# Rounding on ScalarE, subtraction on GpSimd and new places for steps among the products: attention with two expert layers

## The chip, the cores and the metric

The kernel runs on one core of a Trainium2 chip. The metric is the device time of one execution in microseconds (us). Engines are named TensorE (PE, with its weight loads PEld), VectorE (DVE), ScalarE (ACT), GpSimd (POOL) and SyncE (SP, which issues most DMAs).

## The reference

Three stages follow each other; each one's output is the next one's input.

```
scores = scale * q @ k^T                      # 2 batches, 8 heads, 576 positions, head size 64
bias   = -(cum_i - cum_j), capped at 0        # cum: running sum of max(s, 0)
attn   = softmax(causal(scores + bias));  x = attn @ v      -> 1152 tokens x 512

first experts (8, 512->1024->512): each token goes to its best expert (softmax gate, at most
  288 tokens per expert); out = gate * (relu(x w1) w2)
second experts: the (token, expert) logits are served from the highest down, 144 tokens per
  expert, until each token has one; out = relu(x w1) w2
```

## The kernel before

**Attention.** The 16 heads run through a software pipeline written out by hand: one iteration m of a Python loop issues steps of several heads at once, in the order of `ORDER[m % 2]`, one list for even m and one for odd m. Names of steps: `M0` to `M3` (products of scores for the maxima of head m+3), `D0` to `D3` (VectorE takes the row maxima of them, line 485, into `rm`), `G0` (line 490: the five maxima of a row are scaled and rounded to whole numbers by adding and keeping the constant MAGIC), `G1` (line 497: VectorE takes MAGIC and the group references `refb` off, the result is `ng`; GpSimd then splits it into two f16 parts, `NH` at line 400 and `NL` at line 411, in `qb`), `Q` and `QE` (transpose of `qb` for head m+1, `br`), `E0` to `E3` (scores again, then exponentials on ScalarE, line 534, into `pf`), `P0` and `P1` (`ph`, the f16 part of `pf`, on VectorE, line 400; `pl`, the rest, on GpSimd, line 411), `V0` to `V2` (products with v into `pog`), `R0` to `R2` (row sums, reciprocal, scaling: lines 568, 571, 576), `T` and `TE` (transposes of k and q for head m+5, copied out by ScalarE as `al` and `ar`, line 406). Once for each pair of heads come `K`, `QS`, `VS`, `VT` (loads split in f16 parts; the second copy of the f16 part of q, `QD` at line 400, is GpSimd's), `S` (the low parts of k or q, line 438, VectorE) and `X1`, `X`, `XE`, `XG` (the output is split, `XR`, and multiplied with the gate). `D3` comes after `G0`: it reads the rounded `rm` as the start of its maximum (line 485, operand `rm`).

An even iteration holds `QS`, `VT` and the low part of q; an odd one `K`, `VS`, the low part of k and the GpSimd step on `XR`. A pair is one of each. All engines take their instructions in the order of the program.

**Second experts.** The 8 experts run one after the other (`moe2`). Each has a layer 1 (four groups of 24 f16 or bf16 matmuls, lines 904 to 906, each group followed by `relu` on ScalarE, line 915) and a layer 2 (four groups of f32 matmuls, line 1795, read out by ScalarE, line 1801). Which tokens an expert gets is worked out meanwhile, phase by phase, by the generator `work`: one `next(work)` runs one of seven steps of a phase. In short: `rows_of` (five transposes, line 1117, copied to `rowb` by ScalarE, line 1120), three steps of `compare` (ScalarE line 1532 for two of the five tiles, VectorE line 1534 for three), `products` (lines 1524 to 1540) with what follows from them on VectorE, the counts (line 1733, then VectorE from line 1736 on), and the slots (line 1394) with the choice of tokens. `layer1` and `second2` call `tick(k)` at 22 places of an expert (0 to 11 in layer 1, 12 to 21 in layer 2), and the tables `FIRST` (expert 0) and `THEN` (the others) say what is issued there: `w` a step of `work`, `h` the high part of a weight quarter (ScalarE, line 160), `l` its low part (VectorE, line 164), `0` and `1` the two halves of the previous expert's output (transposes at line 1811, ScalarE, a scatter by GpSimd at line 1815), `s` and `t` the two halves of the next expert's gathered input (16 transposes at line 1418, copied by ScalarE and by VectorE at line 1420), `.` nothing. `s` and `rows_of` write the same PSUM bank A0. After the last phase `checks` verifies the result: two multiplications on GpSimd, then eight short VectorE instructions.

Of the kernel before, what the change touches and what calls it, by code (L numbers as in the profile page):

```python
# [9 lines left out]
F32 = mybir.dt.float32  # L10
# [3 lines left out]
AF = mybir.ActivationFunctionType  # L14
OP = mybir.AluOpType
# [6 lines left out]
def tile_attention_moe_moe(ctx: ExitStack, tc: tile.TileContext, q, k, v, s, wg1, w1a, w2a, capacity,  # L22
                           wg2, w1b, w2b, out, dbg=None):
    nc = tc.nc
# [161 lines left out]
    ap = at.enter_context(tc.tile_pool(name="attn", bufs=1))  # L186
# [9 lines left out]
    NH = B * H  # L196
# [38 lines left out]
    RMS = [ap.tile([P, NT], F32, name=f"rm{i}") for i in range(4)]  # L235
# [91 lines left out]

    g1 = sp.tile([P, S], F32, name="g1")
    XB = ap.tile([P, NT, NH], F32, name="XB")
    refb = ap.tile([P, NH, G], F32, name="refb")  # L330

    def groups():
        nc.vector.tensor_scalar(g1[64:96], gi[64:96], 0.0, -1024.0, op0=OP.is_ge, op1=OP.mult)
        for r in (64, 96):
            nc.vector.scalar_tensor_tensor(BLS[0][r:r + 32, :S], gi[64:96], 31.0, g1[64:96], op0=OP.is_le, op1=OP.mult)
        for x in BLS[1:]:
            nc.gpsimd.dma_start(x[64:, :S], BLS[0][64:, :S])

    def references():
        ref8 = sp.tile([NH, G], F32, name="ref8")  # L340
        nc.vector.tensor_scalar(ref8, cum13[:, 0:S:32], 2.0 ** -10, MAGIC, op0=OP.mult, op1=OP.add)
        nc.vector.tensor_scalar(ref8, ref8, MAGIC, None, op0=OP.subtract)
        xrow = ones_row
        nc.vector.scalar_tensor_tensor(xrow.rearrange("e (g w) -> e g w", w=32),
                                       ref8[:, :, None].to_broadcast([NH, G, 32]), -1024.0,
                                       cum13.rearrange("e (g w) -> e g w", w=32), op0=OP.mult, op1=OP.add)
        nc.vector.tensor_copy(refh[:NH], ref8)
        r8l = sp.tile([NH, G], F32, name="r8l")
        nc.vector.tensor_sub(r8l, ref8, refh[:NH])
        nc.vector.tensor_copy(refh[32:32 + NH], r8l)  # L350
        pb = psM.tile([P, NT, NH], F32, name="pM")
        for t in range(NT):
            w = 128 if t < 4 else 64
            nc.tensor.transpose(pb[:w, t], xrow[:, t * P:t * P + w], identf[:NH, :NH])
        pr = psM.tile([P, NH, G], F32, name="pM")
        for h in range(NH):
            nc.tensor.matmul(pr[:, h], selc[:, h:h + 1].to_broadcast([64, P]), refh, start=True, stop=True)
        nc.scalar.activation(XB[:, :4], pb[:, :4], AF.Copy, scale=2.0 ** -13)
        nc.scalar.activation(XB[:64, 4], pb[:64, 4], AF.Copy, scale=2.0 ** -13)
        nc.scalar.activation(refb, pr, AF.Copy)  # L360


    wgh = const.tile([P, 4, 2, E], F16, name="wgh")
# [22 lines left out]
    def raw_copy(o, i):  # L386
# [2 lines left out]
    later = []  # L389

    ENG = dict(KL="DD", QL="DD", BR="DD", AL="AA", AR="AA", XE0="AA", XE1="AA", XH="AA",
               XL="PP", NH="PP", NL="PP", KH="AA", QH="AA", QD="PP", last="DD", PH0="DD", PH1="DD", PL0="PP", PL1="PP",
               VS="DD", VL="PP", VH="AA")

    def copied(name, i, o, x, scale=None):
        e = ENG[name][i % 2]
        if e == "A":
            nc.scalar.activation(o, x, AF.Copy, **({} if scale is None else dict(scale=scale)))
        elif scale is None:
            (nc.gpsimd if e == "P" else nc.vector).tensor_copy(o, x)  # L400
        else:
            (nc.gpsimd if e == "P" else nc.vector).tensor_scalar(o, x, scale, None, op0=OP.mult)
# [7 lines left out]
    def less(name, i, o, x, y):  # L410
        (nc.gpsimd if ENG[name][i % 2] == "P" else nc.vector).tensor_sub(o, x, y)  # L411
# [29 lines left out]
    def heads(m):  # L441
        n, h = divmod(m, 2)
        b, p = divmod(n, NP)
        return n, h, b, 2 * p + h
# [41 lines left out]
                                           r if t == 4 and j0 == 0 else -3e38, OP.add, OP.max, r)  # L486

    def q_dve0(m):
        rm = RMS[m % 4]
        nc.vector.tensor_scalar(rm[:, :NT], rm[:, :NT], 2.0 ** -10, MAGIC, op0=OP.mult, op1=OP.add)  # L490

    def q_dve1(m):
        n, h, b, hh = heads(m)
        rm = RMS[m % 4]
        qb = QB[n % 3]
        ng = aw.tile([P, NT, G], F32, name="ng")
        nc.vector.scalar_tensor_tensor(ng, rm[:, :NT, None].to_broadcast([P, NT, G]), MAGIC,
                                       refb[:, m, None, :].to_broadcast([P, NT, G]),
                                       op0=OP.subtract, op1=OP.subtract)
        copied("NH", m, qb[:, :, h, 64:64 + G], ng)  # L500
        less("NL", m, qb[:, :, h, 96:96 + G], ng, qb[:, :, h, 64:64 + G])

# [12 lines left out]
    def e_pe(m, u):  # L515
# [5 lines left out]
        for t, i0, i1 in EU[u]:  # L521
# [8 lines left out]
            r = OFF[t] + i0 - t * P  # L530
            todo.append((pf[:w, r:r + i1 - i0], o[:w], XB[:w, t, m:m + 1]))
            c += i1 - i0
# [55 lines left out]
    def xr(n, i):  # L588
        XR = XRP[1]
        b, p = divmod(n, NP)  # L590
        return XR[:, b, :, i * DM + p * P:i * DM + (p + 1) * P]

    def x1(n):
        xs = XSS[n % 2].rearrange("p t h d -> p t (h d)")
        copied("XH", n, xr(n, 0), xs)
        less("XL" if n < NPAIR - 1 else "last", n, xr(n, 1), xs, xr(n, 0))

# [147 lines left out]
    for m in range(-7, NH + 3):  # L745
# [51 lines left out]
        if m == -5:  # L797
            references()
# [767 lines left out]
    def pop_lo():  # L1566
        if late:
            split_lo(*late.pop(0))
# [22 lines left out]
    m, Bo = m0, Bo0  # L1591
# [168 lines left out]
    def checks():  # L1760

        nc.gpsimd.tensor_tensor(chk[:, 0], own0[:, 0], own0[:, 0], OP.mult)
        nc.gpsimd.tensor_tensor(chk[:, 1, :CT], SL2, SL2, OP.mult)
        nc.vector.reduce_sum(Q[:, 0, :E], chk[:, 0].rearrange("p t e -> p e t"), axis=AX.X)
        nc.vector.reduce_sum(Q[:, 1, :E], chk[:, 1, :CT].rearrange("p t e -> p e t"), axis=AX.X)
        nc.vector.reduce_sum(dbl[:, 0], BA0, axis=AX.X)
        nc.vector.reduce_sum(dbl[:, 1, :CT], A, axis=AX.X)
        nc.vector.memset(dbl[:, 1, CT:], 0.0)
        nc.vector.tensor_scalar(dbl[:, :2], dbl[:, :2], 1.5, None, op0=OP.is_ge)
        nc.vector.reduce_sum(Q[:, :2, E], dbl[:, :2], axis=AX.X)  # L1770
        nc.vector.tensor_add(Q[:, 2], Q[:, 0], Q[:, 1])
        yield
        pq = px[:, 128:128 + E + 1]
        nc.tensor.matmul(pq, onesf, Q[:, 2], start=True, stop=True)
        nc.vector.tensor_scalar(bad[:, 1, :E], tot, FULL, None, op0=OP.not_equal)
        nc.vector.memset(bad[:, 1, E:], 0.0)
        nc.vector.tensor_tensor(bad[:, 0], pq, expq, OP.not_equal)
        nc.vector.reduce_sum(badf, bad, axis=AX.XY)
        nc.vector.tensor_copy(badi, badf)
        nc.vector.tensor_scalar(badf, badf, 1e6, None, op0=OP.mult)  # L1780
        nc.vector.tensor_scalar(tokl, tok[:, E - 1], badf[:S2], None, op0=OP.add)
# [41 lines left out]
    def moe2(script):  # L1823
        pend = None
        given.difference_update(range(E, 2 * E))
        for e in range(E):
            i0 = 2 * E + 2 * e

            def tick(k, e=e):
                for c in script(e, k):  # L1830
                    if c == "h":
                        pop_hi()
                    elif c == "l":
                        pop_lo()
                    elif c in "01":
                        if pend is not None:
                            back2(*pend, int(c))
                    elif c == "w":
                        next(work, None)
                    elif e + 1 < E:  # L1840
                        XT1[e + 1] = spread(xg[e + 1], XT1.get(e + 1), "st".index(c))
                        if c == "t":
                            del xg[e + 1]
                    load_next()
                    gather_next()

            halved = HALF2 if e else 0
            hs = layer1(mo2, split_ws(i0), XT1.pop(e), CAP2, none, tick, halved)
            pend = (e, second2(i0 + 1, hs, halved, tick), gates[0])
            gates.pop(0)  # L1850
        last = []
        for q_ in range(2):
            back2(*pend, q_, last)
# [14 lines left out]

    FIRST = "w h lw l . 0ww ww . . . . w . ww h . l h wst lh lw1 hll"
    THEN = "w . . . 0 . . ww . w h l1w h wl . h l . swh tl l ."
    FIRST, THEN = (x.split() for x in (FIRST, THEN))
    next(work)
    pop_lo()
# [5 lines left out]
    pop_lo()  # L1881
    moe2(lambda e, k: (THEN if e else FIRST)[k].strip("."))
    assert next(work, None) is None
    bv = nc.values_load(badi[0:1, 0:1], min_val=0, max_val=4 * E)  # L1884
    with tc.If(bv > 0):
# [12 lines left out]
        def again(e, k):  # L1898
            if k == 8 and e + 1 < E:
                xg[e + 1] = gather(tok[:, e + 1])  # L1900
            return THEN[k].strip(".")

# [36 lines left out]
```

## Time and profile before

| | us |
|---|---|
| median of 3 runs | 489.27 (487.54 to 490.25) |
| profiled execution | 487.02 |
| its span, first to last instruction | 485.2 |
| busy: PE, PEld, DVE, ACT, POOL | 413.0, 380.5, 321.1, 244.4, 190.3 |

The attention takes the first 150 us, the products of the first experts run from about 163 to 276 us, those of the second from 327 to 472 us, and the first steps of the second routing lie between. A profiled instruction's line number is that of the kernel; a tile is named without its buffer number.

### The profile page before, as it was taken

Reading aid. Unit: us, or ns where it says so; the run is one execution under the profiler, and the core shown is the slowest. Engines: PE = TensorE matmul, PEld = TensorE weight load, DVE = VectorE, ACT = ScalarE, POOL = GpSimd, SP = SyncE. Lnnn points to the kernel's source line nnn. Section 1 sums busy time; section 2 is a strip of 40 time slices with the busy share of each in tenths; the row PEclk is TensorE's granted clock in tenths of the full one; section 3 lists DMA queues with packets and bytes.
Section 4 is the critical chain, followed back from the end, with each engine's and each line's share of the span. In section 5 each row is a group of like instructions: output and inputs, shape, how many; then the busy total and the mean of one; then the engine's idle time right before and its main releaser. Section 6 shows DMA issues by size and latency. Waiting matters only on the chain. (4 is left out here: it accounts for less than half of the span.)

```text
span 485.2 us, 13714 instructions
## 1 busy us (share of the span) xinstructions
PE 413.0 (85%) x5227; PEld 380.5 (78%) x5227; DVE 321.1 (66%) x949; ACT 244.4 (50%) x441; POOL 190.3 (39%) x299
## 2 busy tenths in 40 slices
PE   1679999977987999999999985649999999998980
PEld 1557778766774799999999985639899899998980
DVE  6799999995865357777778935458773763653300
ACT  3466777743662246545667604225456456454420
POOL 3595667756743503212322700432233322332211
PEclk9999999987987699999999988657999999999995
DMA  8787889749903689999996910449999769689001
GB/s 174 167 202 168 206 194 223 139 139 313 263 3 127 204 238 387 341 345 391 343 344 139 179 25 7 133 121 273 362 333 340 233 192 353 230 287 309 15 26 29
DMA packets 94405, 103.09 MB, mean 212 GB/s; under 512 B 56136, under 2 KB 63304, under 8 KB 94323
## 3 DMA queue, kind: packets, MB, share of 16 engines
q1 hardware_dynamic: 88931, 91.85, 65.3%
q0 software_dynamic: 4192, 9.91, 6.3%
q8 instruction: 45, 0.74, 0.6%
q10 hardware_dynamic: 1200, 0.30, 0.3%
q14 instruction: 37, 0.30, 0.2%
HBM read 81.42 MB, written 14.59 MB: 198 GB/s over the span
## 5 line engine op out<-in xcount | busy, mean ns | idle before, releaser
L164 DVE TENSOR_TENSOR wl<-wf,wh 128x1024 bf16<-128x1024 f32 x62 | 74.7, 1222 | 19.7 <-ACT wh L160 17.5
L160 ACT ACTIVATE wh<-wf 128x1024 f16<-128x1024 f32 x64 | 65.8, 1050 | 12.3 <-DMA wf<-in_moe_w_dram 12.3
L906 PE MATMUL A<-xt,wl 128*128 128x144 f16 (+4 forms) x288 | 61.0, 235 | 0.0
L905 PE MATMUL A<-xt,wh 128*128 128x144 f16 (+4 forms) x288 | 61.0, 235 | 0.0
L904 PE MATMUL A<-xt,wh 128*128 128x144 f16 (+4 forms) x288 | 61.0, 235 | 0.0
L1074 POOL DMA_INDIRECT x2d<-xo,tix x16 | 26.3, 1646 | 81.7 <-DVE l L1090 33.9
L961 PE MATMUL C<-h,wf 128*128 128x160 f32 (+7 forms) x544 | 58.3, 269 | 0.0
L906 PEld LDWEIGHTS <-wl 128*128 128x128 bf16 x512 | 51.8, 101 | 2.6 <-issue 2.6
L904 PEld LDWEIGHTS <-wh 128*128 128x128 f16 x512 | 51.9, 101 | 1.4 <-PE pM L642 1.4
L905 PEld LDWEIGHTS <-wh 128*128 128x128 f16 x512 | 51.7, 101 | 0.9 <-issue 0.4
L534 ACT ACTIVATE pf<-pE,XB 128x512 f32<-128x512 f32 (+4 forms) x80 | 36.9, 514 | 19.7 <-PE pE L529 15.5
L1815 POOL DMA_INDIRECT out_dram<-x2f,tok x14 | 15.7, 1121 | 66.9 <-ACT h L915 37.5
L411 POOL TENSOR_TENSOR pl<-pf,ph 128x512 f16<-128x512 f32 x30 | 35.2, 1186 | 14.3 <-DVE ph L400 12.6
L961 PEld LDWEIGHTS C<-h,wf 128*128 128x128 f32 x256 | 36.2, 190 | 0.0
L1795 PE MATMUL C<-h,wf 128*128 128x144 f32 x256 | 35.3, 290 | 0.0
L485 DVE CUSTOM_DVE_ANT_0 junk<-pM,cb 128x128 f16<-128x128 f32 (+4 forms) x80 | 32.1, 428 | 3.7 <-PE pM L475 3.6
L473 PE MATMUL pM<-al,ar 128*128 128x128 f16 (+2 forms) x96 | 27.4, 326 | 8.0 <-DVE rm L485 5.1
L1795 PEld LDWEIGHTS C<-h,wf 128*128 128x128 f32 x256 | 32.4, 190 | 0.0
L1399 POOL DMA_INDIRECT xg<-x2d,tok x16 | 22.6, 1411 | 22.1 <-PE A L1117 7.2
L557 PE MATMUL pog<-vf,pf 128*128 128x65 f32 x180 | 30.0, 291 | 0.0
L904 PE MATMUL C<-xt,wh 128*128 128x144 f16 x128 | 25.7, 232 | 0.0
L905 PE MATMUL C<-xt,wh 128*128 128x144 f16 x128 | 25.7, 232 | 0.0
(404 smaller groups left out, 1186.9 us busy)
## 6 DMA issues: line engine op xcount, KB each, us to landing
wf<-in_moe_w_dram SPq DMA_DIRECT2D x128, 512.0 KB
xd<-zero SPq DMA_DIRECT2D x18, 257.0 KB
cb<-cumd SPq DMA_DIRECT2D x16, 288.0 KB
x2d<-zero SPq DMA_DIRECT2D x9, 260.5 KB
kf<-in_k_dram SPq DMA_DIRECT2D x16, 128.0 KB
vf<-in_v_dram SPq DMA_DIRECT2D x16, 128.0 KB
qf<-in_q_dram SPq DMA_DIRECT2D x14, 128.0 KB
bl<-al SPq DMA_DIRECT2D x16, 72.0 KB
```

Of the source, the lines that this page charges most:

```text
L160: nc.scalar.activation(hi, src, AF.Copy)
L164: (nc.gpsimd if i == 0 and (0, part) in POOL0 else nc.vector).tensor_sub(lo, src, hi)
L411: (nc.gpsimd if ENG[name][i % 2] == "P" else nc.vector).tensor_sub(o, x, y)
L473: nc.tensor.matmul(o, AR[m][:, t * P:(t + 1) * P], AL[m][:, j0:j1], start=True, stop=not diag)
L485: nc.vector.tensor_tensor_reduce(junk[:w, :j1 - j0], o, CB[m][:w, j0:j1], 1.0, r if t == 4 and j0 == 0 else -3e38, OP.add, OP.max, r)
L534: nc.scalar.activation(d, o, AF.Exp, bias=x, scale=2.0 ** -13)
L557: nc.tensor.matmul(o, pf[:, c:c + P], VF[n % 4][:, j, h], start=False, stop=j == t)
L904: nc.tensor.matmul(ph[:, g], wh[:, c, fs], xt[:, c], start=c == 0, stop=False)
L905: nc.tensor.matmul(ph[:, g], wh[:, c, fs], xt[:, 4 + c], start=False, stop=False)
L906: nc.tensor.matmul(ph[:, g], wl[:, c, fs], xt[:, c], start=False, stop=c == 3)
L961: nc.tensor.matmul(py[:, g], a[:, f, d], b[:, f], start=k == 0, stop=k == len(terms) - 1)
L1795: nc.tensor.matmul(py[:, g], a[:, f, d], b[:, f], start=k == 0, stop=k == len(terms) - 1)
```

## The change

- `G0` becomes an ACTIVATE on ScalarE (Identity with a scale and the per-row operand `magic` as bias). MAGIC is now added to `refb` when that is copied out of PSUM, by VectorE instead of ScalarE.
- `G1` becomes a plain subtraction of `refb` from `rm` on GpSimd.
- The copy `QD` moves from GpSimd to VectorE.
- In the second experts the steps of `work` and some `h` and `l` stand at other ticks. In `checks` a `yield` parts the GpSimd multiplications from the VectorE instructions.

```
+    magic = ap.tile([P, 1], F32, name="magic")
+    nc.vector.memset(magic, MAGIC)
-        nc.scalar.activation(refb, pr, AF.Copy)
+        nc.vector.tensor_scalar(refb, pr, MAGIC, None, op0=OP.add)
-               XL="PP", NH="PP", NL="PP", KH="AA", QH="AA", QD="PP", last="DD", PH0="DD", PH1="DD", PL0="PP", PL1="PP",
+               XL="PP", NH="PP", NL="PP", KH="AA", QH="AA", QD="DD", last="DD", PH0="DD", PH1="DD", PL0="PP", PL1="PP",
     def q_dve0(m):
         rm = RMS[m % 4]
-        nc.vector.tensor_scalar(rm[:, :NT], rm[:, :NT], 2.0 ** -10, MAGIC, op0=OP.mult, op1=OP.add)
+        nc.scalar.activation(rm, rm, AF.Identity, bias=magic, scale=2.0 ** -10)
     def q_dve1(m):
-        nc.vector.scalar_tensor_tensor(ng, rm[:, :NT, None].to_broadcast([P, NT, G]), MAGIC,
-                                       refb[:, m, None, :].to_broadcast([P, NT, G]),
-                                       op0=OP.subtract, op1=OP.subtract)
+        nc.gpsimd.tensor_tensor(ng, RMS[m % 4][:, :NT, None].to_broadcast([P, NT, G]),
+                                refb[:, m, None, :].to_broadcast([P, NT, G]), OP.subtract)
         nc.gpsimd.tensor_tensor(chk[:, 1, :CT], SL2, SL2, OP.mult)
+        yield
         nc.vector.reduce_sum(Q[:, 0, :E], chk[:, 0].rearrange("p t e -> p e t"), axis=AX.X)
-    THEN = "w . . . 0 . . ww . w h l1w h wl . h l . swh tl l ."
+    THEN = "w . . . 0 w w . w . h w1l h wl h . w l s tl h l"
```

In `THEN` the `rows_of` step moves from tick 18 to 16, the second and third `compare` from tick 7 (both) to 5 and 6, `products` from 9 to 8; the counts stay at 11 and the slots at 13. In `FIRST` `rows_of` goes from 5 to 7, the `compare` steps from 6, 6, 11 to 8, 9, 10, `products` and the counts from 13 (both) to 12 and 14, the slots from 18 to 16.

VectorE in an even iteration, from the second `ph` to the low part of q. Before:

```order
L400 CAST ph_163<-pf_161 128x512
L568 TENSOR_SCALAR rs<-pog 128x5
L571 RECIPROCAL rs<-rs 128x5
L490 TENSOR_SCALAR rm_158<-rm_158 128x5
L576 TENSOR_TENSOR xs_167<-pog,rs 128x5x64
L485 ISA junk,rm_158<-pM,cb,rm_158 64x512
L485 ISA rm_158 64x1
L402 TENSOR_SCALAR vf_110<-vf_110 128x10x64
L613 TENSOR_TENSOR LG<-LG,pT 128x32
L613 TENSOR_TENSOR LG<-LG,pT 64x8
L497 SCALAR_TENSOR_TENSOR ng<-rm_158,refb 128x90
L438 SCALAR_TENSOR_TENSOR qb_132<-qf_108,qa 128x10x64
```

And in the changed kernel, whose lines are numbered two or three higher:

```order
L403 CAST ph_163<-pf_161 128x512
L403 COPY qa<-qa 128x10x64
L570 TENSOR_SCALAR rs<-pog 128x5
L573 RECIPROCAL rs<-rs 128x5
L578 TENSOR_TENSOR xs_167<-pog,rs 128x5x64
L488 ISA junk,rm_158<-pM,cb,rm_158 64x512
L488 ISA rm_158 64x1
L405 TENSOR_SCALAR vf_110<-vf_110 128x10x64
L615 TENSOR_TENSOR LG<-LG,pT 128x32
L615 TENSOR_TENSOR LG<-LG,pT 64x8
L441 SCALAR_TENSOR_TENSOR qb_132<-qf_108,qa 128x10x64
```

The rounding and `ng` are gone from the row and the copy of `qa` stands behind the second `ph`. On ScalarE the rounding stands behind the last two exponentials of the iteration and ahead of `al` and `ar`; on GpSimd `ng` stands right ahead of `NH`.

TensorE near the end of expert 1 of the second experts (`xg` is the gathered input, `m` the maxima for `rows_of`, `wf` the weights of layer 2). Before:

```order
L1418 LDWEIGHTS xg
L1418 MATMUL A_9103<-ident,xg 128x72
L1117 MATMUL A_9113<-identf,m_9016 128x128 x3
L1117 MATMUL A_9117<-identf,m_9016 128x128 x2
L1795 MATMUL A_9091<-h,wf_3027 128x144 x4
L1418 LDWEIGHTS xg
```

And in the changed kernel:

```order
L1396 LDWEIGHTS O_8963
L1396 MATMUL px<-R_8964,O_8963 72x16
L1798 MATMUL C_9053<-h,wf_3029 128x144 x8
L1119 MATMUL A_9092<-identf,m_9007 128x128 x3
L1119 MATMUL A_9096<-identf,m_9007 128x128 x2
L1798 MATMUL A_9101<-h,wf_3029 128x144 x8
L1420 LDWEIGHTS xg
L1420 MATMUL A_9114<-ident,xg 128x72
```

The transposes of `rows_of` stood right behind those of `s`; now eight matmuls of layer 2 lie between, and `rows_of` comes first.

VectorE at the end of expert 5 (`chk` is GpSimd's product for the checks, `xt` the next expert's input). Before, and then in the changed kernel:

```order
L164 TENSOR_TENSOR wl_84<-wf_78,wh_83 128x4x256 x2
L1410 COPY gq<-xg 72x2
L1764 TENSOR_REDUCE Q<-chk 128x8
L1765 TENSOR_REDUCE Q<-chk 128x8
L1766 TENSOR_REDUCE dbl<-BA_8093 128x9
L1767 TENSOR_REDUCE dbl<-A 128x5
L1768 MEMSET dbl 128x4
L1769 TENSOR_SCALAR dbl<-dbl 128x18
L1770 TENSOR_REDUCE Q<-dbl 128x2
L1771 TENSOR_TENSOR Q<-Q 128x9
L1420 COPY xt<-A_10357 128x576
L164 TENSOR_TENSOR wl_84<-wf_78,wh_83 128x4x256
```

```order
L164 TENSOR_TENSOR wl_84<-wf_78,wh_83 128x4x256 x2
L1412 COPY gq<-xg 72x2
L1422 COPY xt<-A_10350 128x576
L164 TENSOR_TENSOR wl_84<-wf_78,wh_83 128x4x256
L1767 TENSOR_REDUCE Q<-chk 128x8
```

The copy of `xt` no longer stands behind the sums over `chk`.

## Rows read from the trace of the kernel before

**Rows 1.** Busy time by stretch; columns: PE, PEld, DVE, ACT, POOL, clock, DMA, GB/s.
```profile
71.27:84.90 13.63, 13.02 (x191) 10.97 (x191) 13.56 (x46) 10.52 (x22) 9.43 (x12) 1.00 0.91 211
367.55:386.01 18.46, 17.45 (x231) 17.06 (x229) 10.68 (x39) 10.22 (x17) 5.76 (x6) 1.00 0.82 271
```
**Rows 2.** Instructions of lines 490, 497 and 400: duration ns min/median/max, first and last start.
```profile
L490 DVE TENSOR_SCALAR rm<-rm x16: 130/973/1119, 17.2 to 124.1; 128x5 f32<-128x5 f32 x16
L497 DVE SCALAR_TENSOR_TENSOR ng<-rm,refb x16: 231/238/758, 18.9 to 126.4; 128x90 f32<-128x90 f32 x16
L400 DVE CAST ph<-pf x32: 412/422/1890, 31.8 to 140.2; 128x512 f16<-128x512 f32 x32
L400 POOL COPY qa<-qa x8: 710/718/1386, 7.8 to 89.4; 128x640 f16<-128x640 f16 x8
```
**Rows 3.** Timeline of VectorE, an even, then an odd iteration: start, duration, line.
```profile
74.75 1.12 DVE L490 TENSOR_SCALAR rm<-rm 128x5 f32<-128x5 f32 x1
75.78 0.47 DVE L576 TENSOR_TENSOR xs<-pog,rs 128x320 f32<-128x320 f32 x1
...
77.42 0.24 DVE L497 SCALAR_TENSOR_TENSOR ng<-rm,refb 128x90 f32<-128x90 f32 x1
77.58 0.81 DVE L438 SCALAR_TENSOR_TENSOR qb<-qf,qa 128x640 f16<-128x640 f32 x1
...
81.52 0.97 DVE L490 TENSOR_SCALAR rm<-rm 128x5 f32<-128x5 f32 x1
...
83.47 1.04 DVE L438 SCALAR_TENSOR_TENSOR ka<-kf,ka 128x640 f16<-128x640 f32 x1
```
**Rows 4.** Timeline of GpSimd in the same two iterations.
```profile
74.68 1.16 POOL L411 TENSOR_TENSOR pl<-pf,ph 128x512 f16<-128x512 f32 x1 [0.43 <-DVE rs L568]
...
77.41 1.52 POOL L411 TENSOR_TENSOR vl<-vf,vh 128x256 f16<-128x256 f32 x1 [0.91 <-DVE vf L402]
...
79.21 0.36 POOL L411 TENSOR_TENSOR qb<-ng,qb 128x90 f16<-128x90 f32 x1
80.07 2.39 POOL L411 TENSOR_TENSOR pl<-pf,ph 128x512 f16<-128x512 f32 x2 [0.51 <-DVE ph L400]
82.43 1.40 POOL L411 TENSOR_TENSOR XR<-xs,XR 128x640 f16<-128x640 f32 x1
```
**Rows 5.** Timeline of ScalarE where the odd iteration's rounding will stand.
```profile
80.35 0.81 ACT L534 ACTIVATE pf<-pE,XB 128x320 f32<-128x320 f32 x2
81.64 0.65 ACT L406 ACTIVATE al<-pT 128x576 f16<-128x576 f16 x1 [0.48 <-PE pT L449]
```
**Rows 6.** Timeline of TensorE in the same pair: its two longest waits.
```profile
76.31 0.19 PE L560 MATMUL pog<-vh,ph 128*128 128x65 f16 x1 [0.30 <-DVE xs L576]
...
79.15 0.20 PE L526 MATMUL pM<-br,bl 128*128 128x64 f16 x1 [0.22 <-DVE rm L485]
```
**Rows 7.** Timeline of TensorE in the second experts: instructions that waited.
```profile
341.33 0.27 PE L1733 MATMUL px<-BA,ones 128*128 128x8 f16 x5 [0.76 <-DVE own L1723]
...
364.65 0.54 PE L1117 MATMUL A<-identf,m 128*128 128x128 f32 x3 [0.73 <-ACT xt L1420]
...
377.79 0.31 PE L1394 MATMUL px<-R,O 128*72 128x16 f16 x5 [0.28 <-DVE tot L1736]
...
440.07 0.22 PE L905 MATMUL D<-xt,wh 128*128 128x144 f16 x1 [2.26 <-DVE xt L1420]
```
**Rows 8.** Timeline of TensorE, expert 2: the last of `products`.
```profile
373.86 0.27 PE L1540 MATMUL px<-Bh,g 128*128 128x8 f16 x5
```
**Rows 9.** Timeline of ScalarE, expert 1's weights and expert 2's `compare`.
```profile
345.32 1.06 ACT L160 ACTIVATE wh<-wf 128x1024 f16<-128x1024 f32 x1 [5.62 <-DMA wf<-in_moe_w_dram]
...
372.06 1.54 ACT L1532 ACTIVATE g<-rowb,m 128x640 f16<-128x640 f32 x2
```
**Rows 10.** Timeline of VectorE at the end of expert 5.
```profile
438.36 0.28 DVE L1764 TENSOR_REDUCE Q<-chk 128x8 f32<-128x72 f32 x1 [3.82 <-POOL chk L1762]
...
439.57 0.45 DVE L1420 COPY xt<-A 128x576 f16<-128x576 f16 x1
```

More of the change, by code (lines that the diff above doesn't have):

```diff
@@ L489, in q_dve0 @@
         rm = RMS[m % 4]
-        nc.vector.tensor_scalar(rm[:, :NT], rm[:, :NT], 2.0 ** -10, MAGIC, op0=OP.mult, op1=OP.add)
+        nc.scalar.activation(rm, rm, AF.Identity, bias=magic, scale=2.0 ** -10)
     def q_dve1(m):
         n, h, b, hh = heads(m)
-        rm = RMS[m % 4]
         qb = QB[n % 3]
         ng = aw.tile([P, NT, G], F32, name="ng")
-        nc.vector.scalar_tensor_tensor(ng, rm[:, :NT, None].to_broadcast([P, NT, G]), MAGIC,
-                                       refb[:, m, None, :].to_broadcast([P, NT, G]),
-                                       op0=OP.subtract, op1=OP.subtract)
+        nc.gpsimd.tensor_tensor(ng, RMS[m % 4][:, :NT, None].to_broadcast([P, NT, G]),
+                                refb[:, m, None, :].to_broadcast([P, NT, G]), OP.subtract)
         copied("NH", m, qb[:, :, h, 64:64 + G], ng)
@@ L1867, in gather_next @@
                 passed(999)
-    FIRST = "w h lw l . 0ww ww . . . . w . ww h . l h wst lh lw1 hll"
-    THEN = "w . . . 0 . . ww . w h l1w h wl . h l . swh tl l ."
+    FIRST = "w h wl l . w . w w w w . w . wh l w h st lh wl hll"
+    THEN = "w . . . 0 w w . w . h w1l h wl h . w l s tl h l"
     FIRST, THEN = (x.split() for x in (FIRST, THEN))
```

## Prediction

> **What bounds the kernel now.** I read the busy time by stretch first, to see which engine is full where, then the timelines of VectorE and GpSimd through two heads, those of ScalarE and TensorE at the same place, and last TensorE's waits in the second experts. In a pair of attention heads that lasts 13.63 us VectorE is busy for 13.56, TensorE for 13.02, ScalarE for 10.52 and GpSimd for 9.43 [rows 1]. VectorE sets the pace and TensorE stands close behind it. TensorE's two longest waits there are for VectorE, 0.30 and 0.22 [rows 6]; with the short ones it idles 0.61 of the pair. Ends of matmuls are modelled, and a lone one shows as 0.19 to 0.20 [rows 6], so up to that much of each gap counts as busy: with four gaps TensorE has at least 0.61 and at most 0.61 + 4 x 0.20 = 1.4 to give per pair. The granted clock is 1.00 there, that is 2.4 GHz.
>
> In the second experts TensorE is the bound: 17.45 of 18.46 us in expert 2 [rows 1]. What it loses there are named waits [rows 7], and VectorE at 10.68 and ScalarE at 10.22 of the 18.46 have room. So the change is worth what it takes off VectorE in the attention, as far as TensorE and GpSimd let it through, and what it takes out of TensorE's gaps in the second experts.
>
> **Attention, what VectorE loses and gains.** The rounding runs 16 times. It takes 0.13 at best and 0.973 in the median for five numbers per row [rows 2]: in the odd iteration shown it starts at 81.52 and ends at 82.49, just as GpSimd's two `pl`, begun at 80.07 and 2.39 long, end at 82.46 [rows 3, 4]. So most of its time is waiting for a GpSimd instruction. In the even iteration it holds VectorE from 74.75 to the next start at 75.78, 1.03; in the odd one for some 0.9 of its 0.97, less the same 0.09 that rows overlap. `ng` holds it for 77.58 - 77.42 = 0.16 in each [rows 3]. That is 1.03 + 0.9 + 0.32 = 2.25 per pair. Added is one copy `QD` per pair. The trace shows none of this kind on VectorE: from below 0.13, its shortest instruction here; from above 0.71, GpSimd's time for the same copy; nearest is the cast `ph` with 0.42 for 512 numbers [rows 2]. I take 0.35. It waits for nothing: it stands between the second `ph` and the start of `pl`, when GpSimd is idle for 0.43 [rows 4]. Net 1.9.
>
> Not all of this arrives. In the odd iteration the next VectorE instruction that GpSimd can hold up is the low part of k. It ran from 83.47 and took 1.04, against 0.81 for that of q [rows 3], since `XR` ran on GpSimd from 82.43 to 83.83 [rows 4]. With the rounding gone it arrives 0.9 earlier, at about 82.6, again behind the start of `XR`, and waits for its end as before. So the 0.9 of the odd iteration is given back, and only `ng`'s 0.16 stays. GpSimd has `ng` more and `QD` less; a subtraction of 90 numbers takes it 0.36 [rows 4]. Ahead of the odd iteration's `pl` it idles 0.51, so 0.15 is left, and the cast `ph`, which both want the moment for, may be held up by anything from 0 to 0.36. A pair then gains 1.9 - 0.9 = 1.0 down to 0.64, and TensorE lets through 0.61 to 1.4. I take 0.7, nearer to the lower ends, since both engines must then run with almost no gap.
>
> Heads 1 to 10 are five such pairs: 3.5. The first odd iteration has no `XR` and the last no low part of k, so each keeps 0.9 on VectorE; TensorE lets perhaps 0.3 of that through: 0.6. Head 0, still slowed by GpSimd's fills: 0.8. The three heads ahead of it, where the rounding took near its shortest time, lose 0.1 each by the way over ScalarE: -0.3. The last two heads come behind the first gate, where VectorE is not full: 0. Sum 4.6, taken as 4.5. Above, the ceiling is TensorE: five pairs of 1.4 and 1.0 for the rest, 8. Below, nothing is won and each of 16 heads waits 0.1 on ScalarE: -1.6.
>
> The new wait: `D3` on VectorE now waits for the rounding on ScalarE, and behind `D3` stand the low parts and the next head's maxima. In the odd iteration ScalarE ends its exponentials at 80.35 + 0.81 = 81.16 and idles 0.48 until 81.64 [rows 5]. The maxima are ready before 81.52, where VectorE began its own rounding. The two exponentials took 0.81 together, so I price the rounding at 0.3: it ends by 81.8 at the latest. `D3` follows `xs`, which now starts at 81.52 and lasts 0.47 [rows 3]: 82.0. So it is hidden with 0.2 to spare, and costs its lateness beyond that. Moving `refb` to VectorE happens once, early, and is taken as 0.
>
> **Second experts.** TensorE's waits, with the change that removes each [rows 7]: 0.76 in expert 0, where the counts stood directly behind `products`; 0.73 in experts 1 to 3, where `rows_of` waits until ScalarE has copied `s` out of the same bank (now it comes first, with eight matmuls between); 0.28 in experts 1 to 4, where the slots wait for `tot`, which stood behind a low part of the weights; 2.26 behind expert 5, where the copy of `xt` stood behind the sums that wait 3.82 for GpSimd's `chk` [rows 10]. Sum 0.76 + 3 x 0.73 + 4 x 0.28 + 2.26 = 6.3.
>
> A wait takes their place. `products` moves 12 matmuls forward, and 231 matmuls fill 17.45 us [rows 1], so by about 12 x 0.076 = 0.9. Its last tile stood at 373.86 and would stand at 372.96 [rows 8]; the two `compare` on ScalarE run from 372.06 to 373.60 [rows 9], and ScalarE's order there is unchanged. TensorE waits about 0.6 in each of experts 1 to 4: -2.4. Each of the nine gaps also hides up to 0.2 of a modelled tail, taken as 0.12: +1.1. Sum 6.3 - 2.4 + 1.1 = 5.0. Above: no new wait, 7.4. Below: all but the 2.26 given back, 2.3. The weights are no cover in expert 0: ScalarE waited 5.62 for the first quarter of expert 1's [rows 9]. If they come no sooner, the 0.76 there is lost; the bound takes that in.
>
> **The sum.** 487.02 (the profiled execution) - 4.5 - 5.0 = 477.5. That execution is 2.25 below the median of the runs, so the time compared is 479.8, given as 479.5.
>
> **Rivals.**
>
> A. GpSimd and VectorE hand the time to and fro, and the attention gains nothing. For it: the odd iteration above. In the even one `vl` on GpSimd starts at 77.41, next to `ng` at 77.42; without `ng` the low part of q comes at that moment, and if `vl` went first it would wait between nothing and the whole 1.52, say half, 0.8, which eats the rest of the pair's gain. Against it: at 77.41 VectorE won, `vl` was stretched to 1.52 and the low part kept its 0.81 [rows 3, 4]. Then only the second experts gain: 489.27 - 5.0 = 484.3. The Trainium skill (SBUF — State Buffer, "Who interferes with whom") says that whichever of the two issues first has the shared pair for its whole instruction. By that rule `vl`, first by 0.01, would hold VectorE up and the time would be this rival's 484.3; the row shows the later one served, so the trace does not bear it out at this place.
>
> The Trainium skill (Perfetto Trace Analysis, "Optimizing Scalar/DVE Operations") warns that offloading between GpSimd and VectorE might not help. By it `ng`'s 16 x 0.16 = 2.6 would be void and the time 482.1; no row shows `ng` on GpSimd yet.
>
> B. TensorE waits longer in the second experts: the compares come later still, and only the 2.26 is won: 489.27 - 4.5 - 2.3 = 482.5. For it: ScalarE also holds `relu` and the split of weights. Against it: its order is the same.
>
> C. Slower. The rounding does not get ahead of `al` on ScalarE in time, because the exponentials before it come late by TensorE. Then `D3` waits for it, and VectorE, full as it is, loses that in every head. If ScalarE's work were late by one evacuation (0.65 [rows 5]) and the 0.2 to spare gone with 0.3 more of the other's wait, a head loses 0.75: 16 x 0.75 = 12, and 489.27 + 12 - 5.0 = 496. It turns to slower from (5.0 + 2.4) / 16 = 0.46 per head. Against it: the 0.48 idle, and that ScalarE's chain gets earlier with VectorE's.
>
> **How the numbers follow.** A result within 0.5%, that is 486.8 to 491.7, can't be told from no change. Forecast 0.62, its own range 474.5 to 483.5; A 0.2; B 0.1; C 0.05; both A and B together, near 487, 0.03. The range goes down to what 8 and 7.4 would nearly give, 473.5 (489.27 - 15.4 = 473.9), and up to 487, where A and B meet. Faster: nearly all of the forecast and B and most of A, 0.87; the same 0.08; slower 0.05.
>
> **What would show it.** Right: VectorE's rows without the rounding and a pair near 12.9; the low part of k in odd iterations waiting some 1.1 beyond its 0.81; the rounding on ScalarE ended before `D3`; no wait at `rows_of`, and none of 2.26 behind expert 5; a wait of about 0.6 in `products` of experts 1 to 4. Wrong: VectorE idle ahead of `D3`; `vl` short and the low part of q long; a pair still at 13.6; new waits of layer 1 for ScalarE.

## The result, and the profile after

The changed kernel takes 467.73 us (465.77 to 468.86, 4 runs) against 488.4 for the kernel before in the same comparison: a ratio of 0.9576 (0.9519 to 0.9634). Three more comparisons, on three chips, gave 0.9685 (0.9637 to 0.9733), 0.9594 (0.9543 to 0.9645) and 0.9578 (0.9543 to 0.9613). It is faster, as forecast, but by 20.7 us instead of 9.8, below the lower end of the range.

The profiled execution took 465.77, span 464.0. Busy time by stretch, for two pairs of attention heads and for expert 2 of the second experts, columns as in [rows 1]:

```profile
59.32:71.83 12.51, 12.51 (x201) 10.89 (x197) 11.76 (x43) 10.71 (x26) 10.48 (x13) 1.00 0.87 207
71.83:84.13 12.30, 12.30 (x192) 10.68 (x189) 11.83 (x42) 10.47 (x25) 10.63 (x13) 1.00 0.98 215
349.60:367.20 17.60, 17.29 (x234) 17.08 (x231) 10.59 (x38) 10.16 (x18) 6.38 (x7) 1.00 0.79 265
```

By its rows, whose ends are modelled, TensorE is busy for the whole of both pairs: it is the bound now, and VectorE has 0.47 to 0.75 to spare. A pair went from 13.63 [rows 1] to 12.30 and 12.51 (12.40 between starts of the same matmul), an expert from 18.46 to 17.60.

Instructions of the moved lines (duration ns min/median/max), which answer to [rows 2]:

```profile
L494 ACT ACTIVATE rm<-rm,magic x16: 293/300/303, 16.1 to 114.0; 128x5 f32<-128x5 f32 x16
L500 POOL TENSOR_TENSOR ng<-rm,refb x16: 330/336/857, 17.3 to 117.0; 128x90 f32<-128x90 f32 x16
L403 DVE COPY qa<-qa x8: 313/316/485, 7.8 to 83.5; 128x640 f16<-128x640 f16 x8
L441 DVE SCALAR_TENSOR_TENSOR ka<-kf,ka x8: 810/811/824, 7.0 to 78.8; 128x640 f16<-128x640 f32 x8
```

Timelines of GpSimd and then of VectorE in an odd iteration and the start of the even one, as in [rows 3, 4]:

```profile
53.74 2.37 POOL L414 TENSOR_TENSOR XR<-xs,XR 128x640 f16<-128x640 f32 x1
56.06 0.34 POOL L500 TENSOR_TENSOR ng<-rm,refb 128x90 f32<-128x90 f32 x1
...
57.30 1.16 POOL L414 TENSOR_TENSOR pl<-pf,ph 128x512 f16<-128x512 f32 x1
```

```profile
54.02 0.81 DVE L441 SCALAR_TENSOR_TENSOR ka<-kf,ka 128x640 f16<-128x640 f32 x1
...
57.69 1.06 DVE L403 CAST ph<-pf 128x512 f16<-128x512 f32 x1
58.67 0.31 DVE L403 COPY qa<-qa 128x640 f16<-128x640 f16 x1
```

The low part of k starts 0.28 after `XR` and takes its 0.81. All eight take 0.81 to 0.82, but only three of them come while `XR` runs, 0.28 to 0.36 behind its start; there it is `XR` that grows, from 1.40 [rows 4] to 2.37 and 2.44. `ph` behind `pl`, though, takes 1.06.

TensorE's new waits in the second experts, in place of those of [rows 7]; the line of 0.31 comes four times:

```profile
318.70 0.24 PE L908 MATMUL C<-xt,wl 128*128 128x144 f16 x1 [1.84 <-DVE wl L164]
338.58 0.28 PE L1542 MATMUL px<-Bh,g 128*128 128x8 f16 x5 [0.31 <-ACT g L1534]
342.77 0.39 PE L1798 MATMUL C<-h,wf 128*128 128x144 f32 x1 [0.34 <-ACT h L917]
```

Where the time went, by the starts of the same matmuls in all profiles. The first gate chooses the experts for the tokens of the first batch, the second gate for those of the second. "To the gate" is from the first `pog` to the first gate's `pT<-OH,before` (mostly heads 0 to 10), "gate" from there to `pE<-ka,XR` of the second gate, "routing" from `D<-IW,wtl` to the first matmul with the second experts' `xt`, "second" from there to the last of layer 2:

| profile | to the gate | gate | routing | second |
|---|---|---|---|---|
| before | 71.73 | 48.64 | 49.17 | 143.57 |
| before, again (e8) | 71.11 | 48.25 | 47.03 | 146.72 |
| changed | 64.46 | 43.24 | 45.40 | 138.30 |
| changed, again (e5) | 64.49 | 48.55 | 46.32 | 138.22 |
| changed, third (e10) | 64.45 | 44.56 | 44.91 | 138.08 |
| changed, fourth (e15) | 64.45 | 44.65 | 44.91 | 138.38 |
| e1 attention part | 64.45 | 43.18 | 46.01 | 143.88 |
| e2 second experts' part | 71.76 | 48.34 | 46.06 | 137.85 |
| e3 filler at the gate | 71.09 | 44.57 | 46.76 | 144.47 |
| e4 fillers in the changed kernel | 64.50 | 44.52 | 51.46 | 139.12 |
| e6 rounding only | 72.13 | 48.11 | 47.83 | 146.01 |
| e7 tables retimed | 66.17 | 47.02 | 47.02 | 138.20 |
| e9 QD back | 64.82 | 48.76 | 48.94 | 148.33 |
| e11 ng only | 69.91 | 48.59 | 46.11 | 143.97 |
| e12 yield only | 71.09 | 48.25 | 46.76 | 141.55 |
| e13 head 14 moved | 72.29 | 45.47 | 50.37 | 145.58 |
| e14 head 14 back | 65.52 | 45.54 | 46.48 | 138.39 |

Between the first two profiles that is -7.27, -5.40, -3.77 and -5.27; with +1.43 ahead of them, -0.52 between the second gate and the first experts and -0.21 in these it makes the 21.0 by which TensorE ends earlier. The first and the last column repeat to a few tenths in all four profiles of the changed kernel. (e7, with the same attention, has 66.17 because its first `pog` comes 1.5 earlier than the changed kernel's and the next ones wait 1.85 for `pl`; its gate begins at 100.05, the changed kernel's at 99.80.) The two in the middle do not repeat, and they are what the experiments are mostly about.

### The profile page after: what moved, and what is told of

Read it like the earlier page. It is cut to its first block, busy times and chain, and to the rows that moved or that the text cites. A ratio compares the mean times of both kernels' runs of the same rounds, so it can differ in the third digit from the quotient of the medians.

```text
span 464.0 us, 13688 instructions
## 1 busy us (share of the span) xinstructions
PE 401.2 (86%) x5227; PEld 372.8 (80%) x5227; DVE 311.4 (67%) x927; ACT 246.8 (53%) x456; POOL 193.7 (42%) x307
## 5 line engine op out<-in xcount | busy, mean ns | idle before, releaser
L907 PE MATMUL A<-xt,wh 128*128 128x144 f16 (+4 forms) x288 | 59.5, 231 | 0.0
L908 PE MATMUL A<-xt,wl 128*128 128x144 f16 (+4 forms) x288 | 59.5, 231 | 0.0
L906 PE MATMUL A<-xt,wh 128*128 128x144 f16 (+4 forms) x288 | 59.5, 231 | 0.0
L908 PEld LDWEIGHTS <-wl 128*128 128x128 bf16 x512 | 50.8, 99 | 2.2 <-DVE wl L164 2.0
L906 PEld LDWEIGHTS <-wh 128*128 128x128 f16 x512 | 50.9, 99 | 1.0 <-PE pM L644 1.0
L907 PEld LDWEIGHTS <-wh 128*128 128x128 f16 x512 | 50.7, 99 | 0.9 <-issue 0.4
L1818 POOL DMA_INDIRECT out_dram<-x2f,tok x14 | 16.8, 1200 | 63.7 <-ACT h L917 35.6
L1401 POOL DMA_INDIRECT xg<-x2d,tok x16 | 21.2, 1328 | 22.4 <-DVE xt L1422 6.2
L559 PE MATMUL pog<-vf,pf 128*128 128x65 f32 x180 | 28.7, 282 | 0.0
L908 PE MATMUL C<-xt,wl 128*128 128x144 f16 x128 | 24.6, 226 | 1.8 <-DVE wl L164 1.8
L907 PE MATMUL C<-xt,wh 128*128 128x144 f16 x128 | 24.6, 226 | 0.0
```

The costliest lines, as they stand in the source:

```text
L559: nc.tensor.matmul(o, pf[:, c:c + P], VF[n % 4][:, j, h], start=False, stop=j == t)
L906: nc.tensor.matmul(ph[:, g], wh[:, c, fs], xt[:, c], start=c == 0, stop=False)
L907: nc.tensor.matmul(ph[:, g], wh[:, c, fs], xt[:, 4 + c], start=False, stop=False)
L908: nc.tensor.matmul(ph[:, g], wl[:, c, fs], xt[:, c], start=False, stop=c == 3)
```

## The experiments

**Which part brings what.** e1 takes only the hunks of the attention from the diff, e2 only the two tables and the `yield`.

> The attention part of the change alone (rounding on ScalarE, ng on GpSimd, QD on VectorE), the second experts as before. Measured so far: 488.4 to 467.7, of which the traces put about 6 into heads 1 to 10, about 5 into the heads around the first gate, 1 behind them, 4 to 5 into the second routing and 5.3 into the second experts. Theory 1 (TensorE's clock): what lies around the first gate and in the second routing comes from shorter stretches at 1.2 GHz that follow from TensorE being fuller in the attention; most of it comes with this part: 472 to 477, with the stretch from the wait for OH to head 11 near 7.5 instead of 12. Theory 2 (moved work alone): only the pairs of heads get shorter, 481 to 482. Theory 3 (chance of one execution): the gate and the routing come out as before in this profile or differ without pattern, 476 to 484.

> The second experts' part alone (the two tables and the yield), the attention as before. All theories: 488.4 - 5.3 = 483 from the second experts. Theory 1: gate stretch as before (about 12 from the wait for OH to head 11), clock there at 1.2 GHz for 6 or more; total 482 to 484. Theory 3: the second routing, whose instructions neither part touches, may again be 4 to 5 shorter: 478 to 483. If e1 and e2 together give less than the 20.7 of the whole change, the rest is tied to both.

e1: ratio 0.9762 (0.9728 to 0.9796). e2: 0.9891 (0.9853 to 0.9928). Together 0.9656. The second experts gain 5.7 with e2 and nothing with e1, the heads 7.3 with e1 and nothing with e2; the gate's gain comes with the attention part, in one profile of each. e1's 472.82 lies in theory 1's range.

**TensorE's clock.** Around the gate the first two profiles differ in the granted clock. Before, TensorE idles 3.49 for `OH`, and then runs at 1.2 GHz (0.50) up to 111.5 and, behind another wait, from 115.0 to 118.5:

```profile
105.00:111.50 6.50, 5.86 (x53) 4.64 (x53) 5.04 (x31) 0.90 (x2) 3.60 (x5) 0.50 0.52 181
111.50:115.00 3.50, 1.08 (x12) 0.88 (x12) 0.79 (x2) 1.72 (x5) 3.19 (x4) 0.97 0.97 240
115.00:118.50 3.50, 3.39 (x17) 2.31 (x17) 1.61 (x7) 0.78 (x3) 2.15 (x2) 0.52 1.02 411
```

```profile
115.11 0.58 PE L473 MATMUL pM<-al,ar 128*128 128x512 f16 x1 [2.53 <-ACT pf L534]
```

In the changed kernel it idles 2.92 and is at 1.2 GHz once:

```profile
99.50:103.00 3.50, 3.20 (x33) 2.43 (x34) 3.06 (x20) 0.69 (x1) 1.34 (x3) 0.51 0.57 204
103.00:107.30 4.30, 4.22 (x53) 3.36 (x52) 3.54 (x18) 2.79 (x7) 3.38 (x4) 1.00 0.77 194
```

e3 fills that gap in the kernel before with matmuls whose result nobody reads, e4 four such gaps in the changed one. The lines that e3 adds, cut down to the loop:

```
+        for _ in range(0 if b else 60):
+            nc.tensor.matmul(pr[:, 128:256], ident, ident, start=True, stop=True)
```

> The kernel before with 60 extra matmuls (128x128, into an unused part of a PSUM tile) in front of the first gate's matmuls, where TensorE waits 3.49 for OH; about 60 x 0.053 = 3.2 of work in a gap of 3.5. Nothing else is changed. Theory 1: TensorE's clock does not fall there, or later and for shorter; from the wait for OH to head 11 it takes 7 to 9 instead of 12.2, and the time is 483 to 485. Theory 2: the clock has no part in it, 488 to 489 (the filler hides in the gap). If the filler starts late or runs at 1.2 GHz it costs up to 3: 491.

> The changed kernel with the same kind of filler in four of TensorE's waits: 50 matmuls ahead of the first gate (wait 2.92), 42 ahead of the overflow branch of the second routing (2.40), 85 ahead of L1656 (4.83), 58 ahead of the first transposes of the second experts (3.36). Theory 1: the stretches at 1.2 GHz from 99.5 to 103, 284 to 290.5 and 297.5 to 314.5 get shorter or go; TensorE is busy for about 3.2, 6.3 and 9 in them, so up to half of that, 9, can be won: 460 to 465. Theory 2: 467 to 468, or slower by what the fillers overrun (1 to 3).

e3's gate shrank to 44.57, and head 10 to 11 took 10.34 at 2.4 GHz throughout:

```profile
104.75:115.09 10.34, 9.67 (x146) 8.46 (x146) 9.70 (x49) 4.01 (x10) 5.48 (x9) 1.00 0.55 173
```

So the clock can be the price there. Yet the whole got no faster, rather slower: 1.0054 (1.0011 to 1.0097); its one profile does not say why. e4 came out above every comparison of the changed kernel: 0.9822 (0.9779 to 0.9866). Its filler at the gate left TensorE at 2.4 GHz there too, and the gate took 44.52. Its filler ahead of L1656 writes to a PSUM tile that VectorE still read:

```profile
302.40 6.57 PE L1656 MATMUL px<-ident 128*128 128x128 f16 x85 [5.02 <-DVE tot L1645]
```

It began only when the wait was over and then stood in the way for 6.57: the routing took 51.46. That misplaced filler says nothing on the theory.

**The same kernels again.**

> The changed kernel unaltered, beside the kernel before on the same chip as the three runs below, and with a second profiled execution. e1 gave a ratio of 0.976 for the attention part and e2 0.989 for the second experts' part; together 0.965. If the parts add up, the ratio is 0.963 to 0.968; if the whole is more than its parts, 0.958 as in the first comparison. In the profile: pairs of 12.3 to 12.5 again, 43 to 44 from the first gate's matmuls to the second gate's products; from IW,wtl to R,O of the second routing 28 again if that stretch is a matter of the kernel, up to 32 if of the single execution.

> The kernel before, unaltered, timed against itself and profiled a second time. Theory 3 (the clock of a single execution): pairs of 13.6 and second experts of 143.6 again, but from the first gate's matmuls to the second gate's products anything from 43 to 49 (48.6 in the first execution) and from IW,wtl to R,O 28 to 32 (32.1 in the first). Theory 1 (the change shortens these stretches): 48 to 49 and 32 again. Ratio 1.000, with an interval that shows what chance alone does.

> The changed kernel, unaltered, a third time. The parts that repeated so far, 7.3 of the heads up to the first gate and 5.3 of the second experts, make 12.6 or a ratio of 0.974; the two comparisons gave 0.958 and 0.969. Theory 3: between 0.958 and 0.974, with one of the two sizes around the first gate (43 or 48.5). Theory 1: 0.958 to 0.965 and 43 to 44 around the gate.

e5 0.9685, e10 0.9594, e8 0.9992 (0.9957 to 1.0027). In e5 the gate took 48.55 with the changed kernel, in e10 44.56: not every execution has its gain there. e8's gate repeats at 48.25, as theory 1 has it, but its routing is 2.1 shorter and its second experts 3.2 longer than in the first profile of the same kernel. e5's ScalarE and TensorE at the gate:

```profile
105.31 0.84 ACT L536 ACTIVATE pf<-pE,XB 128x64 f32<-128x64 f32 x2 [3.92 <-remote]
...
108.35 0.31 ACT L536 ACTIVATE pf<-pM,XB 64x64 f32<-64x64 f32 x1 [1.57 <-remote]
```

```profile
108.71 0.58 PE L476 MATMUL pM<-al,ar 128*128 128x512 f16 x1 [2.64 <-ACT pf L536]
```

The clock is at 1.2 GHz from 98.2 to 105.0, and the exponentials wait for signals whose sender the profile doesn't show. The first profile of before has the same picture. But e8 has 1.2 GHz for half as long there and still 48.25. VectorE, GpSimd and TensorE of e8 behind the gate:

```profile
115.73 4.12 DVE L490 TENSOR_SCALAR rm<-rm 128x5 f32<-128x5 f32 x1
119.77 0.48 DVE L576 TENSOR_TENSOR xs<-pog,rs 128x320 f32<-128x320 f32 x1
```

```profile
115.23 0.93 POOL L688 DMA_INDIRECT xd<-XR,slot  x1 [0.30 <-issue]
116.17 2.29 POOL L411 TENSOR_TENSOR pl<-pf,ph 128x512 f16<-128x512 f32 x2
118.40 1.41 POOL L411 TENSOR_TENSOR XR<-xs,XR 128x640 f16<-128x640 f32 x1
```

```profile
120.30 0.19 PE L560 MATMUL pog<-vh,ph 128*128 128x65 f16 x1 [3.10 <-DVE xs L576]
```

The rounding of head 14, five numbers per row, takes 4.12 (below: the hold): GpSimd, late by its five scatters, runs two `pl` and `XR` without a gap, and the rounding ends as `XR` ends (119.81). It took 4.12 in e12 too, 3.09 in e2 and 3.35 in e11; 0.13 in the first profile, where TensorE was late instead, and in e3, where `ng` behind it was held.

**That one rounding.** e13 moves rounding and `ng` of head 14 alone in the kernel before, e14 puts them back in the changed one. e14's edit (the statement of `ng` goes on unchanged):

```
+        if m == 14:
+            nc.vector.tensor_scalar(rm[:, :NT], rm[:, :NT], 2.0 ** -10, MAGIC, op0=OP.mult, op1=OP.add)
+            return
-        nc.gpsimd.tensor_tensor(ng, RMS[m % 4][:, :NT, None]
+        (nc.vector if m == 14 else nc.gpsimd).tensor_tensor(ng, RMS[m % 4][:, :NT, None]
```

> The kernel before, with the rounding of head 14 alone on ScalarE and its ng alone on GpSimd: that is the rounding behind the first gate, which took 4.12, 4.12, 3.09 and 3.35 in four second profiles of kernels that have it on VectorE, because GpSimd there runs two pl and XR one behind the other after its five scatters. Theory G (this one rounding is the price around the gate): the stretch from the first gate's matmuls to the second gate's products goes from 48.1 to 48.6 (six executions) to 43 to 46, and the ratio is 0.992 to 0.995. Theory C (TensorE's clock alone decides there): 48 again, ratio 0.999.

> The changed kernel, with rounding and ng of head 14 alone back on VectorE. Theory G: the stretch around the gate is 47 to 49, as in the kernel before, and the time 2 to 4 above the changed kernel's in the same call. Theory C: the stretch has its two sizes (43 to 45, 47 to 49) as in the changed kernel, and the times are equal.

> The changed kernel unaltered, as the measure for e14 on the same chip. Ratio to before 0.958 to 0.969 as in three comparisons.

e13: 0.9953 (0.9929 to 0.9977), gate 45.47, where the five profiles with that rounding in place and no filler have 48.25 to 48.64 (e6, with only `ng` in place, 48.11). e14: 471.15 against 467.0 for e15, ratios 0.9648 (0.9614 to 0.9682) and 0.9578 (0.9543 to 0.9613), which do not overlap, if only just. In e14's profile the rounding got through (0.22), and `ng` behind it was caught, until `XR` was done:

```profile
107.13 0.22 DVE L495 TENSOR_SCALAR rm<-rm 128x5 f32<-128x5 f32 x1
108.57 3.79 DVE L503 TENSOR_TENSOR ng<-rm,refb 128x90 f32<-128x90 f32 x1
```

```profile
108.59 2.29 POOL L414 TENSOR_TENSOR pl<-pf,ph 128x512 f16<-128x512 f32 x2
110.81 1.42 POOL L414 TENSOR_TENSOR XR<-xs,XR 128x640 f16<-128x640 f32 x1
```

So one head's rounding and `ng` on VectorE cost 2 us (e13) to 4 us (e14) of the whole time. Theory G had these times about right, and e13's gate, but not e14's: 45.54 and not 47 to 49. Between the profiles of e14 and e15, 3.82 apart, only 0.89 lie at the gate, 1.07 ahead of it and 1.57 in the routing. And e3, with `ng` held, has 44.57:

```profile
116.35 3.42 DVE L497 SCALAR_TENSOR_TENSOR ng<-rm,refb 128x90 f32<-128x90 f32 x1
```

Neither theory is enough by itself. Sorted by what the first 25 us of the gate show, the 17 profiles have gates of

- 43.18 to 45.47 with at most one stretch at 1.2 GHz and no hold (the changed kernel but for e5; e1, e4, e13);
- 44.57 and 45.54 with the hold and no such stretch ahead of it (e3, e14);
- 48.25 to 48.59 with the hold behind such a stretch (e8, e12; e2 and e11, which then have a second stretch);
- 47.02 to 48.76 with two such stretches and no hold (before, e5, e6, e7, e9).

So at the gate the hold goes with some 3 behind a stretch at 1.2 GHz (e8 against e13) and about 1 without one (e14 against e4). This order was found in the profiles afterwards; no run tests it, and what brings on a second stretch is open.

**The three edits of the attention apart.** e6 is the kernel before with only the rounding moved, e11 with only `ng`, e9 is e1 with `QD="PP"`.

> Of the attention part only the rounding on ScalarE; ng stays on VectorE and QD on GpSimd. Theory A (the rounding's wait for GpSimd was the price): VectorE loses 1.03 + 0.9 per pair, and nearly all arrives, up to TensorE's ceiling: the pair goes to 12.4 to 12.6 and the ratio is about 0.978, nearly that of e1. Theory B (my prediction's account): in the odd iteration the 0.9 is given back before the low part of k, only 1.03 of a pair arrives, the low part of k takes over 1.5 there, the pair is 12.7 to 12.9, the ratio 0.985.

> Of the attention part only ng on GpSimd; rounding on VectorE, QD on GpSimd. Theory A2 (the wait for GpSimd goes to the next VectorE instruction that GpSimd can hold up: in e6 that was ng, 1.45 and 0.63 long, and with ng gone none is left): with the rounding still on VectorE it keeps its 1.0, and only ng's own 2 x 0.16 goes: the pair is 13.2 to 13.4 and the ratio about 0.996. Rival: ng was the costly one by itself: pair 12.5 to 12.8, ratio 0.985.

> The attention part alone, but with the copy QD left on GpSimd. Theory A: TensorE is the bound in the pairs, VectorE has 0.7 of room after the change, so the 0.31 that QD costs VectorE is hidden; on GpSimd it adds 0.72 to 10.6 of 12.3, hidden too: the same ratio as e1, 0.976. Rival: with ng and QD both GpSimd becomes late with pl, the pairs get 0.2 to 0.5 longer, and the ratio is 0.979 to 0.983.

e6: 0.9961 (0.9932 to 0.999); e11: 0.9966 (0.9928 to 1.0004); e9: 0.991 (0.9876 to 0.9944). A pair of heads in e6, in e11 and in e15 (both moved):

```profile
63.26:76.66 13.40, 12.89 (x195) 10.85 (x192) 13.19 (x44) 11.12 (x25) 10.84 (x12) 1.00 0.84 202
```

```profile
56.93:70.39 13.46, 13.10 (x195) 11.09 (x193) 13.39 (x44) 10.46 (x23) 10.74 (x14) 1.00 0.86 200
```

```profile
71.27:83.67 12.40, 12.40 (x195) 10.78 (x193) 11.83 (x42) 10.62 (x26) 10.69 (x13) 1.00 1.00 230
```

Alone the two edits take 0.23 and 0.17 off a pair of 13.63, together 1.23 (e15 also moves `QD`; e9, which does not, has 12.39). Where the rounding's wait goes in e6, VectorE and then GpSimd:

```profile
70.66 0.81 DVE L440 SCALAR_TENSOR_TENSOR ka<-kf,ka 128x640 f16<-128x640 f32 x1
71.39 1.45 DVE L499 SCALAR_TENSOR_TENSOR ng<-rm,refb 128x90 f32<-128x90 f32 x1
```

```profile
70.30 2.44 POOL L413 TENSOR_TENSOR XR<-xs,XR 128x640 f16<-128x640 f32 x1
```

The low part of k passes `XR`; `ng` behind it waits for `XR`'s end (1.45 for 0.24, and 0.63 in the even iteration). With `ng` gone too, nothing that small stands there to be held. Both theories on e6 fell: A put nearly the whole gain on the rounding, B put the wait on the low part of k. e11 came out as theory A2 has it (0.996; its pair, 13.46, just above 13.2 to 13.4). On `QD` both forecasts fell (0.976; 0.979 to 0.983). In the pairs its place makes little difference: 12.40 in e9 by the same matmuls, 12.60 in the last two, against 12.40 in e1. Yet e9's ratio is worse than e1's beyond both intervals. The two stand in different comparisons; in e9's own, the changed kernel (e5) spent 48.55 at its gate too, and of the 14.8 between the profiles of e5 and e9 10.1 lie in the second experts, which e9 has as before and where its clock fell, and 2.6 in the routing. Whether the place of `QD` costs anything outside the pairs stays open.

**The second experts.** e12 is the kernel before with the `yield` alone. e7 is the changed kernel with `lw` for `wl` at tick 2 of `FIRST` and `products` at tick 9 in `THEN`.

> Only the yield in checks, so that the copy of xt comes ahead of the sums over chk. TensorE's wait of 2.26 behind expert 5 goes, the others stay: second experts from 143.6 to 141.3, ratio 0.995. In two profiles without the yield TensorE fell to 1.2 GHz right behind that wait (at 439.0 and 438.3); where that would have happened, the yield gains 1.7 more. Rival: the sums then stand behind the copy and hold up a low part of the weights: nothing gained.

> The changed kernel with two entries of the tables altered: in FIRST tick 2 the low part of the weights ahead of the step of work (lw for wl), in THEN products back at tick 9. TensorE's wait of 1.84 for wl in expert 0 and the four waits of 0.31 in products of experts 1 to 4 should go: 3 less than the changed kernel, ratio 0.006 lower. Rival: the counts then come late (a wait of 0.3 to 0.8 for own or tot as in the kernel before) and in expert 0 the compare is late instead; then nothing is gained.

e12: 0.9937 (0.9906 to 0.9968), second experts 141.55, as forecast. The wait of 2.26 has a follow-up, which e8 shows: TensorE falls to 1.2 GHz right behind it.

```profile
442.34 0.22 PE L905 MATMUL D<-xt,wh 128*128 128x144 f16 x1 [2.25 <-DVE xt L1420]
```

```profile
443.40:446.80 3.40, 3.40 (x32) 3.40 (x30) 0.89 (x8) 0.41 (x1) 0.00 (x0) 0.51 1.04 284
```

Of eight profiles with that wait, the four that fell (e6, e8, e9, e13) took 145.6 to 148.3 for the second experts, the other four (before, e1, e3, e11) 143.6 to 144.5. With the `yield`, in nine profiles, neither shows. e7: 0.9636 (0.9598 to 0.9673) beside 0.9685 for the changed kernel in the same comparison, but the intervals overlap, and its second experts take 138.20 as before: the waits of 1.84 and 0.31 are gone, and expert 1's gathered input is late instead.

```profile
335.34 0.21 PE L1420 MATMUL A<-ident,xg 72*128 72x72 f16 x1 [0.68 <-DMA xg<-x2d,tok]
336.79 0.40 PE L1420 MATMUL A<-ident,xg 72*128 72x72 f16 x7 [1.25 <-DMA xg<-x2d,tok]
```

None of these runs is surely faster than the changed kernel.

## Why the prediction was wrong, by its own steps

- **Right: the bounds and the small prices.** The rounding on ScalarE 0.300 (0.3 forecast), `QD` on VectorE 0.316 (0.35), `ng` on GpSimd 0.336 (0.36), `D3`'s new wait nearly hidden: VectorE idled for it twice, 0.7 in all. Rival C did not come, nor A: in the even iteration the low part of q keeps its 0.81 (median 809 ns).
- **Wrong: "the low part of k ... waits for its end as before", so that the odd iteration's 0.9 is given back.** The low part passes `XR` (0.81, not some 1.1 more). The instruction that inherits the wait is `ng` (1.45 in e6), and the change had moved it as well. VectorE lost 1.73 to 1.80 of busy time per pair, near the 1.9 that I had before that step, and not 0.64 to 1.0. TensorE let 1.12 to 1.33 through, inside the 0.61 to 1.4 stated. The attention up to the gate: -5.8 between the first two profiles, -7.3 from the first `pog` on (that `pog` came 1.4 later), against -4.6.
- **Wrong: the heads behind the first gate at 0.** I read one execution, where head 14's rounding took 0.13 because TensorE was late. In four other profiles it took 3.1 to 4.1; e13 prices it at 2 of the whole time, and of e14's 4 only 0.9 is seen at this place. The 5.40 between the first two profiles goes not with that hold but with the second stretch at 1.2 GHz, 115.0 to 118.5, and the wait of 2.53 ahead of it; the sum had no term for either. The term's bound was taken from the rows of the steady pairs. What stood ahead of the rounding on GpSimd, five scatters, two `pl` and `XR`, was readable in that trace.
- **Right in sum, in part by luck: the second experts**, -5.0 forecast, -5.3 to -5.7 measured (-8.4 against e8, where the clock fell). The wait for the compares is 0.31, not 0.6, which gives back 1.2 in four experts; the wait of 1.84 for `wl` in expert 0 (0.66 to 1.13 in the three later profiles) was not foreseen and takes about as much, nor was it foreseen that the clock sometimes falls behind the wait of 2.26.
- **Not in the sum: the second routing**, 3.77 less between the first two profiles with the same instructions. Over all profiles but e4 it is 46.1 to 50.4 with the old attention and 44.9 to 48.9 with the new one. Mostly this is the single execution; whether one or two us belong to the change stays open.
- **The range** ended at 473.5, because its lower end held TensorE's ceiling in the pairs and nothing for the gate and the routing. Of the 21.0 by which TensorE ended earlier, 9.2 lie in these two.

The Trainium skill (SBUF — State Buffer, "Who interferes with whom") says that a VectorE instruction with two inputs in SBUF contends with a GpSimd instruction that reads SBUF, and that whoever issues first keeps the shared pair to its end. `ng` behind `XR` (1.45) has two such inputs and agrees. `ph` behind `pl` (1.06) and the rounding (4.12) have only one; the same section of the Trainium skill counts casts and `tensor_scalar` among those that can contend, in a two-port mode; no trace here shows whether these ran in one. The low part of k, with two inputs and 0.28 to 0.36 behind the start of `XR`'s row, does not agree: it took 0.81, and `XR` was drawn out to 2.37 and 2.44. Here the measurement decides; it may be that `XR`'s row begins before it reads, which no run here tested.

## What to carry to other kernels

Where a short VectorE instruction shows a long time because GpSimd holds it up, moving it away can hand the wait to the next VectorE instruction that GpSimd can hold up, as it did here: find that one first, and move both or neither (0.23 and 0.17 alone, 1.23 together). Bound such a wait by what can stand in GpSimd's queue at that place, not by the durations of one execution. And where TensorE idles for some us ahead of dense work, look at the granted clock behind it in more than one profile before that stretch is put into a sum, either way.

## What the runs showed of the hardware

- A VectorE instruction on five numbers was held for 4.12 over three GpSimd instructions that followed each other without a gap (e8); it was not let in between them.
- In e5, with TensorE at 1.2 GHz up to 105.0, ScalarE waited 3.92 and 1.57 for signals that come later than the rows of the matmuls before them end; so it did in the first profile of before. What delays them is open.
- The same kernel on the same inputs spent 43.2, 44.6, 44.7 and 48.6 around the gate in four profiles, with the clock at 1.2 GHz at different moments each time.
